# Top-k attention and two gated products: weight halves through PSUM, and an order with other costs

## The chip, the cores and the metric

One core of one Trainium2 chip runs the whole program. The metric is the device time of an execution in microseconds; a kernel's time is the median of its runs. Engines are named as the profile names them: PE (TensorE), DVE (VectorE), ACT (ScalarE), POOL (GpSimd), SP (the queue that issues the DMAs).

## The reference

```python
# q, k, v: 4 batches x 8 heads x 576 positions x 64, float32
scores = q @ k.T / sqrt(64)
kth    = 32nd largest of each row of scores           # top_k = 32
scores = where(scores >= kth, scores, -1e9)
attn   = softmax(scores)
x      = (attn @ v), heads side by side               # 2304 tokens x 512
h = x @ w_in;  g = h * sigmoid(1.702 * h);  x2 = g @ w_out        # 512 -> 2048 -> 512
a = x2 @ w1;  b = x2 @ w2;  out = ((a * b) @ w3) @ w_out2         # 512 -> 1024 -> 1024 -> 512
```

The weights arrive as 64-bit floats, the tensors q, k and v as 32-bit ones.

## The kernel before

The 2304 tokens are 18 tiles of 128 rows. A tile has 8 heads of attention, and then the two gated blocks ("the MoE part" of the code), whose products are all done with numbers split into two 16-bit halves, hi and lo: a product of two such numbers is three 16-bit matmuls, hi by hi, hi by lo and lo by hi (lines 488 to 490).

A head: four matmuls fill a score tile `s_ps` (line 706; two such tiles exist). DVE then finds the 32 largest of 576 by four MAX8 (line 728) with three MATCH_REPLACE8 between them (line 731). ACT masks and exponentiates (746, 749) with a bias `nb` from POOL or DVE (738), writes the hi half (755), POOL writes the lo half (758, 759), a DMA transposes both, and nine matmuls multiply with v (769). ACT and DVE add the halves into `xsb` (809, 813). At the end of a tile the row sums are inverted: three small DVE steps, `+1e-9` (854), reciprocal (855) and a multiplication with the scale of v (834); then `x mul` (838) scales the rows.

The weights have to be made ready first, while the first tiles' heads run. There are 72 blocks of 128 x 512: 8 of w4 (the second w_out), 16 of w3, 16 of w_in, 16 of w_out, 16 of w1 and w2. For each, a DMA brings the 64-bit words (356), ACT takes them apart in three steps (361, 371 or on POOL 366, 375), and DVE joins the words into 32-bit numbers (379, "the join": two inputs in SBUF). The Gram product of the blocks (406), its diagonal (416) and a sum (421) give one scale per matrix, six in all. Then each block is multiplied with the scale and split into halves. For 56 blocks `split_op` does it: the hi half on ACT (313), POOL (330) or DVE (316), the lo half on DVE (323, two inputs in SBUF) or on POOL in two steps (326, 327). The 16 blocks of w1 and w2 lie where their halves go, so `split_in_place` goes through a tile `fsb` (451 or 454, then 457 or 460, then 463 or 466). The halves of w3 are transposed and multiplied with those of w4 into w34 (538, 541 make its halves).

PSUM has three general banks, the pool `mm`. Products, Gram products and the small sums take one each from it.

The order of the instructions on each engine is fixed when the program is built. `Order.run` is a list scheduler: every operation has a cost, a due time and the engines it may run on; operations that are ready are taken by due time; a slot of a pool (a PSUM bank, a buffer) is taken and given back. It runs through time with `GAP` between an operation and its user on another engine, `SAME` on the same engine, and `DMA` for a transfer's flight. On the chip each engine then works through its own list strictly in that order, and waits at the head of it.

Of the kernel before, what the change touches and what calls it, by code (L numbers as in the profile page):

```python
# [35 lines left out]
class Order:  # L36
# [4 lines left out]
    GAP = 0.25  # L41
    SAME = {"T": 0.0, "V": 0.11, "A": 0.12, "G": 0.1, "D": 0.25}
    DMA = 2.3

    def __init__(self):
        self.ops = []
        self.pools = {}
        self.busy = {}
# [4 lines left out]
    def op(self, alts, due, deps=(), env=None, acq=(), rel=(), tag=""):  # L53
        o = Op()
        o.alts, o.prio = alts, due
# [11 lines left out]
    def run(self, log=None):  # L67
        engs = "TVAGD"
        free = dict.fromkeys(engs, 0.0)
        used = dict.fromkeys(engs, 0.0)  # L70
# [9 lines left out]
        while n < len(self.ops):  # L80
# [6 lines left out]
            while ends and ends[0][0] <= now:  # L87
                _, _, o = heapq.heappop(ends)
                for u in o.users:
# [3 lines left out]
                    u.ready = max(u.ready, o.end + (self.SAME[o.eng] if same else self.GAP))  # L93
# [5 lines left out]
            for e in engs:  # L99
                if free[e] > now:  # L100
                    continue
                best = None
                for c in cand[e]:
# [3 lines left out]
                    if best is not None and (o.prio, o.seq) >= (best[0].prio, best[0].seq):  # L107
                        continue
# [5 lines left out]
                    if ok:  # L114
                        best = c
# [13 lines left out]
                free[e] = now + a[1]  # L129
                used[e] += a[1]  # L130
                o.end = now + a[1] + (self.DMA if e == "D" else 0.0)
                for name, env, key in o.rel:
                    t = o.end + self.GAP
                    self.pools[name].append((t, o.seq, env[key]))
                    heapq.heappush(events, t)
# [17 lines left out]
NB_DVE = 1.0  # L153
SIGN_G = 0.5
# [7 lines left out]
def kernel(  # L162
# [38 lines left out]
    ident = mem([P, P], BF16, "ident")  # L201
# [87 lines left out]
    def dve_chain(due, fns, deps=(), env=None, acq=(), rel=(), tag=""):  # L289

        o = None
        for i, f in enumerate(fns):
            first, last = i == 0, i == len(fns) - 1
            o = dve(
                0.09, due, f, deps=deps if first else [o], env=env, acq=acq if first else [], rel=rel if last else [], tag=tag
            )
# [11 lines left out]
    def split_op(due, hi, lo, src, sc, n, deps, env, rel, acq=(), tag="", lo_dve=2.0):  # L308
# [23 lines left out]
        o = op([("A", 0.09 + 0.52 * k, f_hi, 0.0), ("G", 0.12 + 0.57 * k, f_hi_g, HI_G), ("V", 0.1 + 0.6 * k, f_hi_v, lo_dve)], due, deps=deps, env=env, acq=acq, tag=tag + "hi")  # L332
        alts = [("V", 0.1 + 0.9 * k, f_lo_v, lo_dve)]
        if lo_dve > 0.0:
            alts.append(("G", 0.4 + 1.5 * k, f_lo_g, 0.0))
# [12 lines left out]
    def load64(dst, src, raw_pool, deps):  # L348
# [34 lines left out]
        ld = dma(1.5, due - 20, f_load, deps=deps, env=E, acq=[raw_pool], tag="w load")  # L383
        lo = act(0.69, due, f_low, deps=[ld], tag="w low")
        sg = op([("A", 0.55, f_sign_a, 0.0), ("G", 0.9, f_sign, SIGN_G)], due, deps=[lo], tag="w sign")
        mn = act(0.57, due, f_main, deps=[ld, sg], tag="w main")
        return dve(0.87, due, f_join, deps=[sg, mn], env=E, rel=[raw_pool], tag="w join")
# [49 lines left out]

    def split_to(w, i, src, sc, deps):
# [5 lines left out]
    def split_in_place(w, i, sc, deps):  # L444
# [23 lines left out]
        a = op([("V", 0.67, f_v, 0.0), ("A", 0.61, f_a, 0.5)], due, deps=deps, env=E, acq=["f"], tag="w tmp")  # L468
        b = op([("A", 0.52, h_a, 0.0), ("V", 0.42, h_v, 1.0)], due, deps=[a], tag="w hi")
        return op([("G", 1.2, l_g, 0.0), ("V", 0.9, l_v, 1.5)], due, deps=[b], env=E, rel=["f"], tag="w lo")  # L470
# [4 lines left out]
    def transpose_op(due, src, acq, dep, env, n=8):  # L475
# [3 lines left out]
        return dma(1.0, due, f, deps=[dep], env=env, acq=[acq], rel=["h"], tag="T")  # L479
# [21 lines left out]
    def weights():  # L501
# [3 lines left out]
        sp4 = [split_to(wout, 8 + i, block(wout, i), s4, [d4]) for i in range(8)]  # L505
# [10 lines left out]
        for f in range(8):  # L516
# [3 lines left out]
            for kc in range(2):  # L520
                e = {}
                src = block(win, 2 * f + kc)
                s = split_op(
                    due, lambda e=e: e["h"][:, 0:C], lambda e=e: e["h"][:, C : 2 * C], lambda src=src: src, s3, C,
                    [d3], e, [], acq=["h"], tag="w3 ", lo_dve=W_DVE,
                )
# [19 lines left out]
        ready["win"] = [split_to(win, i, block(w12, i), si, [di] + sp3) for i in range(16)]  # L546
# [4 lines left out]
        ready["wout"] = [split_to(wout, i, block(w12, i), so, [do] + cout + pr) for i in range(16)]  # L551
# [5 lines left out]
        ready["w12"] = [split_in_place(w12, i, (s1, s2)[i // 8], [(d1, d2)[i // 8]]) for i in range(16)]  # L557
# [36 lines left out]
    def kv_prep(b, hp, is_v):  # L594
# [54 lines left out]
        kready[b, hp] = [dma(2.0, due, f_t, deps=[m, r], env=E, acq=["kt"], rel=["h", "kr"], tag="k T")]  # L649
# [4 lines left out]
    def q_prep(t):  # L654
# [33 lines left out]
        tr = dma(1.0, due, f_t, deps=[m], env=E, acq=[("q", E, "qa")], rel=["h"], tag="q T")  # L688
        qready[t] = [dma(1.3, due, f_swap, deps=[tr], env=E, acq=[("q", E, "qb")], tag="q swap")]


    def head(t, h, X):
# [87 lines left out]
        if first and j == 0:  # L780
            X["esc", hp] = pool(1.1 * len(pt), due - 6, f_esc(hp, hp + 1), deps=[s], tag="esc")
        elif h == 0:
            o = pool(1.1 * len(pt), due - 6, f_esc(0, NPAIR), deps=[s] + [d for b, _, _, _ in pt for i in range(NPAIR) for d in kready[b, i]], tag="esc")
# [3 lines left out]
        for i in range(3):  # L787
# [4 lines left out]
            [("G", 0.41, f_nb(nc.gpsimd), 0.0), ("V", 0.18, f_nb(nc.vector), NB_DVE)], due - 6, deps=[d, X["esc", hp]],  # L792
# [4 lines left out]
        lo = pool(1.5, due + 7, f_lo, deps=[hi], env=E, rel=["y"], tag="a lo")  # L797
        tr = dma(1.1, due + 8, f_t, deps=[lo], env=E, acq=["at"], rel=["hl"], tag="a T")
# [20 lines left out]
    def tile_end(t, X):  # L819
# [9 lines left out]
        def f_r():  # L829
            for b, s0, r0, n in pt:  # L830
# [3 lines left out]
                nc.vector.tensor_tensor(r2, r2, vi, op=ALU.mult)  # L834
# [15 lines left out]
        def f_t():  # L850
            nc.sync.dma_start_transpose(out=X["t"], in_=X["h"])

        f_rs = [
            lambda: nc.vector.tensor_scalar(r, X["x"][:, :, D], 1e-9, None, op0=ALU.add),
            lambda: nc.vector.reciprocal(r, r),
# [241 lines left out]
```

## Time and profile before

| what | value |
|---|---|
| time, median of 3 runs | 1158.55 us (1156.67 to 1162.78) |
| profiled execution | 1158.71 us, its span 1156.9 us |
| PE, DVE, ACT, POOL busy | 950.6, 960.4, 824.5, 847.8 us |
| first MAX8 of the first head | 19.9 us from the span's start |
| the last weight half | about 337 us |
| the last head's last MAX8 on DVE | about 1060 us |

The table's shares are means over three stages with different limits: up to about 337 us the weights are prepared beside the first heads, up to about 1060 us heads and MoE parts run side by side, and what is left is the MoE part of the last two tiles. A busy PE is not PE at its peak, since a matmul's time includes its way through the array: the distance between two starts tells what it occupies.

### The profile page before, as it was taken

Reading aid. Unit: us, or ns where it says so; the run is one execution under the profiler, and the core shown is the slowest. Engines: PE = TensorE matmul, PEld = TensorE weight load, DVE = VectorE, ACT = ScalarE, POOL = GpSimd, SP = SyncE. Lnnn points to the kernel's source line nnn. Section 1 sums busy time; section 2 is a strip of 40 time slices with the busy share of each in tenths; the row PEclk is TensorE's granted clock in tenths of the full one; section 3 lists DMA queues with packets and bytes.
Section 4 is the critical chain, followed back from the end, with each engine's and each line's share of the span. In section 5 each row is a group of like instructions: output and inputs, shape, how many; then the busy total and the mean of one; then the engine's idle time right before and its main releaser. Section 6 shows DMA issues by size and latency. Waiting matters only on the chain. (4 is left out here: it accounts for less than half of the span.)

```text
span 1156.9 us, 18481 instructions
## 1 busy us (share of the span) xinstructions
PE 950.6 (82%) x5654; PEld 493.7 (43%) x5654; DVE 960.4 (83%) x2112; ACT 824.5 (71%) x1555; POOL 847.8 (73%) x1142
## 2 busy tenths in 40 slices
PE   2335784556869899999889998989999999999996
PEld 1223342323435445544444544544455455555442
DVE  4887795998999888889898898899999999997311
ACT  6977769768777776877678776767868787776421
POOL 4987796657778878878688886858798787686320
PEclk9999996676979999999899998989999999999998
DMA  8959968466835846677668756666765756657331
GB/s 245 299 134 245 218 163 222 114 150 162 172 56 119 149 103 127 118 143 127 122 116 154 124 113 129 118 110 123 128 136 109 146 110 131 112 96 117 71 59 36
DMA packets 428739, 156.95 MB, mean 136 GB/s; under 512 B 406624, under 2 KB 414816, under 8 KB 428640
## 3 DMA queue, kind: packets, MB, share of 16 engines
q1 hardware_dynamic: 428640, 155.78, 65.0%
q8 instruction: 44, 0.72, 0.3%
q14 instruction: 55, 0.45, 0.1%
HBM read 52.43 MB, written 4.72 MB: 49 GB/s over the span
## 5 line engine op out<-in xcount | busy, mean ns | idle before, releaser
L728 DVE MAX8 m8s<-wsb 128x8 f32<-128x576 f32 x432 | 323.5, 754 | 5.4
L731 DVE MATCH_REPLACE8 wsb<-m8s,wsb 128x576 f32<-128x576 f32 x288 | 213.7, 742 | 0.0
L488 PE MATMUL mm<-w,tsb 128*128 128x512 f16 x432 | 167.9, 389 | 16.4 <-DMA tsb<-hsb 16.3
L488 PEld LDWEIGHTS <-tsb 128*128 128x128 f16 x1072 | 106.5, 99 | 156.6 <-DMA tsb<-hsb 47.1
L759 POOL TENSOR_TENSOR hlb<-ysb,hlb 128x512 f16<-128x512 f32 x144 | 168.1, 1168 | 0.0
L489 PE MATMUL mm<-w,tsb 128*128 128x512 f16 x432 | 167.4, 387 | 0.0
L490 PE MATMUL mm<-w,tsb 128*128 128x512 f16 x432 | 166.7, 386 | 0.0
L490 PEld LDWEIGHTS <-tsb 128*128 128x128 f16 x1072 | 106.7, 100 | 132.6 <-issue 10.6
L769 PE MATMUL av<-v2s,ats 128*128 128x130 f16 (+1 forms) x1440 | 114.1, 235 | 49.5 <-DMA ats<-hlb 40.4
L489 PEld LDWEIGHTS <-tsb 128*128 128x128 f16 x1072 | 106.6, 99 | 110.9 <-issue 13.1
L488 PE MATMUL mm<-wout,tsb 128*128 128x512 f16 x352 | 136.1, 387 | 19.7 <-DMA tsb<-hsb 16.7
L728 DVE MAX8 m8s<-s_ps 128x8 f32<-128x576 f32 x144 | 108.8, 756 | 47.4 <-PE s_ps L706 38.9
L746 ACT ACTIVATE s_ps<-s_ps,m8s 128x576 f32<-128x576 f32 x144 | 102.4, 711 | 54.7 <-DVE m8s L728 45.8
L749 ACT ACTIVATE ysb<-s_ps,nbs,asm 128x576 f32<-128x576 f32 x144 | 119.6, 831 | 28.3 <-DVE nbs L738 13.5
L490 PE MATMUL mm<-wout,tsb 128*128 128x512 f16 x352 | 136.0, 386 | 0.0
L489 PE MATMUL mm<-wout,tsb 128*128 128x512 f16 x352 | 135.9, 386 | 0.0
L769 PEld LDWEIGHTS <-ats 128*128 128x128 f16 (+1 forms) x1440 | 97.3, 108 | 82.9 <-DMA ats<-hlb 53.2
L706 PE MATMUL s_ps<-kts,qts 128*128 128x288 f16 (+1 forms) x640 | 106.8, 312 | 30.8 <-ACT ysb L749 24.7
L488 PE MATMUL mm<-win,tsb 128*128 128x512 f16 x288 | 112.4, 390 | 5.6 <-DMA tsb<-hsb 3.1
L489 PE MATMUL mm<-win,tsb 128*128 128x512 f16 x288 | 112.0, 389 | 0.0
L490 PE MATMUL mm<-win,tsb 128*128 128x512 f16 x288 | 111.8, 388 | 0.0
L918 POOL TENSOR_TENSOR fsb<-fsb 128x512 f32<-128x512 f32 x68 | 88.2, 1298 | 29.4 <-ACT fsb L909 27.1
(194 smaller groups left out, 1877.4 us busy)
## 6 DMA issues: line engine op xcount, KB each, us to landing
w<-in_moe_w_dram SPq DMA_DIRECT2D x16, 512.0 KB, 5.3
wout<-in_moe_w_in_dram SPq DMA_DIRECT2D x16, 512.0 KB, 5.3
wout<-in_moe_w_out_dram SPq DMA_DIRECT2D x16, 512.0 KB, 4.7
qts<-qts SPq DMA_DIRECT2D x36, 128.0 KB, 2.6
out_dram<-fsb SPq DMA_DIRECT2D x18, 256.0 KB, 2.4
w<-in_moe_w_out_dram SPq DMA_DIRECT2D x8, 512.0 KB, 5.0
psb<-in_moe_w_dram SPq DMA_DIRECT2D x8, 512.0 KB, 4.6
tsb<-in_moe_w_dram SPq DMA_DIRECT2D x8, 512.0 KB, 5.1
```

The source lines that it names most:

```text
L488: nc.tensor.matmul(o, a[:, i, :], hi, start=(first and i == 0), stop=False)
L489: nc.tensor.matmul(o, a[:, i, :], lo, start=False, stop=False)
L490: nc.tensor.matmul(o, a[:, 4 + i, :], hi, start=False, stop=(last and i == 3))
L706: nc.tensor.matmul(E["sp"][r : r + n, i], qe[q_][:, h, r : r + n], kt[:, j, i * HS : (i + 1) * HS], start=k_ == 0, stop=k_ == 1,)
L728: nc.vector.max(out=E["m8"][:, 8 * i : 8 * i + 8], in_=E["sp"] if i == 0 else E["w"])
L731: nc.vector.match_replace(out=two(E["w"]) if i == 0 else E["w"], in_to_replace=E["m8"][:, 8 * i : 8 * i + 8], in_values=E["sp"] if i == 0 ...
L746: nc.scalar.activation(E["sp"], E["sp"], AF.Prelu, bias=E["m8"][:, TOPK - 1 : TOPK], scale=-1.0, alpha=1.0 / FAR)
L749: nc.scalar.activation(two(E["y"]), E["sp"], AF.Exp, bias=E["nb"], scale=nesc)
L759: nc.gpsimd.tensor_tensor(hl()[:, S + SR : 2 * S], E["y"][:, 0:SM], hl()[:, 0:SM], op=ALU.subtract)
L769: nc.tensor.matmul(X["av", hp][r : r + n, j], E["at"][:, i, r : r + n], v2[:, j, blk, :], start=(i == 0), stop=(i == 8))
L918: nc.gpsimd.tensor_tensor(E["f"], E["f"], E["f2"], op=ALU.mult)
```

## The change

Four things are changed.

1. `split_pe` is new. It multiplies a block of a weight with an identity matrix of 32-bit floats, so that the block itself stands in a PSUM bank; ACT writes the hi half from there, and DVE the lo half. `PEP` names the matrices that go this way: all five, 72 blocks. `ident` becomes a 32-bit tile for it.
2. The three small steps of the row sums go to three engines: `+1e-9` to ACT, the reciprocal stays on DVE, the multiplication with v's scale goes to POOL.
3. `Order.run` knows a lock. Operations of POOL, and those of DVE that are marked with `od.two`, share it: one that starts while it is held is taken to last longer by what is left, and while choosing, such an operation's due time is put back by `LOCK` times that rest.
4. The costs, the gaps by engine and the flight times of DMAs that the scheduler calculates with are other numbers, so the whole order is another.

```diff
-    GAP = 0.25
+    GAP = {"T": 0.25, "V": 0.16, "A": 0.16, "G": 0.1, "D": 0.05}
-    DMA = 2.3
+    DMA = 2.1
...
+                    both = e == "G" or (e == "V" and a[2] in self.both)
+                    mine = (o.prio + (LOCK * max(lock - now, 0.0) if both else 0.0), o.seq)
...
+                cost = a[1]
+                if e == "G" or (e == "V" and a[2] in self.both):
+                    cost += max(lock - now, 0.0)
+                    lock = now + cost
...
+LOCK = 8.0
+PE_DUE, PE_OUT = 100.0, 20.0
+PEP = ("w4", "w3", "win", "wout", "w12")
...
-    ident = mem([P, P], BF16, "ident")
+    ident = mem([P, P], F32, "ident")
...
-        ld = dma(1.5, due - 20, f_load, deps=deps, env=E, acq=[raw_pool], tag="w load")
+        ld = dma(1.3, due - 20, f_load, deps=deps, env=E, acq=[raw_pool], tag="w load", lat=3.6)
...
-        return dve(0.87, due, f_join, deps=[sg, mn], env=E, rel=[raw_pool], tag="w join")
+        return dve(0.65, due, od.two(f_join), deps=[sg, mn], env=E, rel=[raw_pool], tag="w join")
...
+    def split_pe(hi, lo, src, sc, due, deps, env=None, acq=()):
+        E = {} if env is None else env
+        def f_in():
+            nc.tensor.matmul(E["mm"], ident, src(), start=True, stop=True)
+        def f_hi():
+            nc.scalar.activation(hi(), E["mm"], AF.Copy, scale=sc)
+        def f_lo():
+            nc.vector.scalar_tensor_tensor(lo(), E["mm"], sc, hi(), op0=ALU.mult, op1=ALU.subtract)
+        a = pe(0.87, due - PE_DUE, f_in, deps=deps, env=E, acq=["mm"] + list(acq), tag="w in")
+        h = act(0.58, due - PE_OUT, f_hi, deps=[a], tag="w hi")
+        return dve(0.66, due - PE_OUT, f_lo, deps=[h], env=E, rel=["mm"], tag="w lo")
...
-                nc.vector.tensor_tensor(r2, r2, vi, op=ALU.mult)
+                nc.gpsimd.tensor_tensor(r2, r2, vi, op=ALU.mult)
...
+        a = act(0.2, due, lambda: nc.scalar.activation(r, X["x"][:, :, D], AF.Copy, bias=1e-9), deps=r_in, tag="r")
+        a = dve(0.15, due, lambda: nc.vector.reciprocal(r, r), deps=[a], tag="r")
+        a = pool(0.3 * len(pt), due, f_r, deps=[a], tag="r")
...
-        lo = pool(1.5, due + 7, f_lo, deps=[hi], env=E, rel=["y"], tag="a lo")
-        tr = dma(1.1, due + 8, f_t, deps=[lo], env=E, acq=["at"], rel=["hl"], tag="a T")
+        lo = pool(1.42, due + 7, f_lo, deps=[hi], env=E, rel=["y"], tag="a lo")
+        tr = dma(1.35, due + 8, f_t, deps=[lo], env=E, acq=["at"], rel=["hl"], tag="a T")
```

The other lines of the diff are numbers of the same kind.

In the new program the instructions of `split_pe` stand at lines 459 (PE), 462 (ACT) and 465 (DVE), the join at 395, MAX8 at 782, MATCH_REPLACE8 at 785, the score matmuls at 760, the matmuls with v at 823, the lo half of w34 at 590, the row sums at 908 (ACT), 909 (DVE) and 888 (POOL).

DVE where the halves of w_in are made, before (`w_70` is the tile of the 32-bit blocks of w_in, `win` and `wout` are those of the halves, `w_71` is w34):

```order
191 L731 MATCH_REPLACE wsb<-m8s,s_ps_94 128x576
192 L316 TENSOR_SCALAR win<-w_70,wsm 128x512 x4
193 L541 SCALAR_TENSOR_TENSOR w_71<-mm_97,w_71 128x512
194 L316 TENSOR_SCALAR win<-w_70,wsm 128x512
195 L323 SCALAR_TENSOR_TENSOR win<-w_70,wsm,win 128x512
196 L813 TENSOR_TENSOR xsb<-xsb,av 128x2x64
197 L323 SCALAR_TENSOR_TENSOR win<-w_70,wsm,win 128x512 x3
198 L541 SCALAR_TENSOR_TENSOR w_71<-mm_99,w_71 128x512
199 L323 SCALAR_TENSOR_TENSOR win<-w_70,wsm,win 128x512 x6
200 L379 SCALAR_TENSOR_TENSOR w_70<-wout,w_70 128x512 x2
```

Fifteen halves stand there with no MAX8 or MATCH_REPLACE8 between them. And now, where the same halves are made:

```order
246 L465 SCALAR_TENSOR_TENSOR win<-mm_97,wsm,win 128x512
247 L782 MAX m8s<-wsb 128x8
248 L785 MATCH_REPLACE wsb<-m8s,s_ps_95 128x576
249 L465 SCALAR_TENSOR_TENSOR win<-mm_98,wsm,win 128x512
250 L465 SCALAR_TENSOR_TENSOR win<-mm_99,wsm,win 128x512
251 L782 MAX m8s<-wsb 128x8
252 L465 SCALAR_TENSOR_TENSOR win<-mm_97,wsm,win 128x512
253 L785 MATCH_REPLACE wsb<-m8s,wsb 128x576
254 L465 SCALAR_TENSOR_TENSOR win<-mm_98,wsm,win 128x512
255 L395 SCALAR_TENSOR_TENSOR w_70<-wout,w_70 128x512
```

All 16 lo halves are on DVE now, their source is a bank (`mm`), and head steps and joins stand between them.

PE at the same place of the new order, where the blocks of w_in come into the banks (`mm_97`, `mm_98` and `mm_99` are the three banks; before, PE had nothing to do with these blocks beyond their Gram product):

```order
1112 L760 MATMUL s_ps_95<-kts,qts 128x288
1113 L459 MATMUL mm_98<-w_70,ident 128x512
1114 L459 MATMUL mm_99<-w_70,ident 128x512
1115 L459 MATMUL mm_97<-w_70,ident 128x512
1116 L459 MATMUL mm_98<-w_70,ident 128x512
1117 L459 MATMUL mm_99<-w_70,ident 128x512
1118 L459 MATMUL mm_97<-w_70,ident 128x512
1119 L823 LDWEIGHTS ats
1120 L823 MATMUL av<-v2s,ats 128x130
```

Six blocks stand in a row over three banks, and a head's matmuls with v behind them: the fourth can start only when DVE has given back the first one's bank.

DVE at the row sums of the first tile, before:

```order
163 L813 TENSOR_TENSOR xsb<-xsb,av 128x2x64
164 L854 TENSOR_SCALAR asm<-xsb 128x8
165 L379 SCALAR_TENSOR_TENSOR w_70<-wout,w_70 128x512
166 L855 RECIPROCAL asm<-asm 128x8
167 L316 TENSOR_SCALAR hsb<-win,wsm 128x512
168 L834 TENSOR_TENSOR asm<-asm,kvinv 128x8
```

Now only the reciprocal is in DVE's list:

```order
156 L867 TENSOR_TENSOR xsb<-xsb,av 128x2x64
157 L785 MATCH_REPLACE wsb<-m8s,wsb 128x576
158 L909 RECIPROCAL asm<-asm 128x8
159 L782 MAX m8s<-wsb 128x8
160 L395 SCALAR_TENSOR_TENSOR w_70<-wout,w_70 128x512
```

Counted over the whole lists: when the sixth scale is formed on DVE (the diagonal of w2, the last matrix), 25 heads have been begun on DVE before, and 31 now; the last weight half on DVE comes after 32 begun heads. The signs of the 64-bit words are on ACT for 62 blocks before and for 48 now, the rest is on POOL. Of the 144 `nb` steps DVE has 64 before and 53 now. SP's list has as many DMAs as before. Of the 16 halves of w3, 11 go through the bank `mm_97`.

## Rows read from the trace of the kernel before

**Rows 1.** The page, busy time of each engine
```profile
PE 950.6 (82%) x5654; PEld 493.7 (43%) x5654; DVE 960.4 (83%) x2112; ACT 824.5 (71%) x1555; POOL 847.8 (73%) x1142
```

**Rows 2.** Windows: stretch, its us, busy us (instructions) by engine, PEclk, DMA share, GB/s
```profile
core 0: us, PE busy (x) PEld busy (x) DVE busy (x) ACT busy (x) POOL busy (x), PEclk, DMA share, GB/s
0.00:337.00 337.00, 188.02 (x1086) 101.95 (x1087) 277.86 (x545) 260.58 (x475) 251.48 (x302) 0.86 0.74 185
337.00:1060.00 723.00, 679.10 (x4179) 354.49 (x4177) 663.06 (x1527) 532.98 (x1021) 571.43 (x810) 0.97 0.66 123
848.00:1060.00 212.00, 207.03 (x1329) 109.90 (x1326) 202.99 (x457) 159.17 (x294) 164.37 (x231) 1.00 0.64 120
1060.00:1157.00 97.00, 83.49 (x393) 37.28 (x390) 19.47 (x43) 30.95 (x61) 24.87 (x31) 0.96 0.32 60
83.00:143.00 60.00, 38.86 (x234) 20.05 (x234) 44.77 (x90) 44.93 (x75) 41.83 (x50) 0.97 1.02 224
214.00:270.00 56.00, 28.93 (x161) 15.72 (x160) 52.91 (x102) 37.49 (x69) 42.48 (x53) 0.65 0.64 154
```

**Rows 3.** Waits of DVE from 337 to 1060: us, times, longest us
```profile
DVE m8s L728 <- PE s_ps L706: 31.7, 28, 3.8
```

**Rows 4.** DVE busy us up to 337, weight halves: L316, L323, L451, L460, L466
```profile
0.00:337.00 337.00, 13.87 (x18) 0.86 0.74 185
...
0.00:337.00 337.00, 30.63 (x25) 0.86 0.74 185
...
0.00:337.00 337.00, 7.87 (x11) 0.86 0.74 185
...
0.00:337.00 337.00, 2.76 (x4) 0.86 0.74 185
...
0.00:337.00 337.00, 1.98 (x3) 0.86 0.74 185
```

**Rows 5.** Groups by line: engine, op, out<-in, count | busy us, mean ns | idle
```profile
L541 DVE SCALAR_TENSOR_TENSOR w<-mm,w 128x512 f16<-128x512 f32 x8 | 5.4, 680 | 0.8 <-ACT w L538 0.8
...
L953 DVE SCALAR_TENSOR_TENSOR hsb<-mm,msm,hsb 128x512 f16<-128x512 f32 x18 | 13.3, 740 | 2.7 <-ACT hsb L950 2.7
...
L323 DVE SCALAR_TENSOR_TENSOR wout<-w,wsm,wout 128x512 f16<-128x512 f32 x10 | 13.2, 1386 | 0.0
```

**Rows 6.** DVE up to 337, the joins (L379)
```profile
0.00:337.00 337.00, 65.86 (x72) 0.86 0.74 185
```

**Rows 7.** The joins of w_in and w_out: duration ns min/median/max, first and last start
```profile
L379 DVE SCALAR_TENSOR_TENSOR w<-wout,w x32: 666/687/1798, 91.0 to 211.7; 128x512 uint32<-128x512 uint32 x32
```

**Rows 8.** Groups by line on DVE: row sums and the bias of the exponent
```profile
L854 DVE TENSOR_SCALAR asm<-xsb 128x8 f32<-128x8 f32 x18 | 13.3, 739 | 0.0
...
L834 DVE TENSOR_TENSOR asm<-asm,kvinv 128x8 f32<-128x8 f32 (+1 forms) x20 | 6.5, 327 | 0.1
...
L738 DVE TENSOR_SCALAR nbs<-m8s,asm 128x1 f32<-128x1 f32 x64 | 16.7, 262 | 0.7
```

**Rows 9.** Timeline, DVE: start us, us, what
```profile
330.13 3.90 DVE L854 TENSOR_SCALAR asm<-xsb 128x8 f32<-128x8 f32 x1
```

**Rows 10.** Timeline, POOL in the same stretch
```profile
331.63 1.15 POOL L463 TENSOR_TENSOR w<-fsb,w 128x512 f16<-128x512 f32 x1
332.75 1.25 POOL L995 TENSOR_TENSOR psb<-psb,fsb 128x512 f32<-128x512 f32 x1
```

**Rows 11.** Timeline, PE after the last head, two neighbours
```profile
1079.98 0.38 PE L489 MATMUL mm<-w,tsb 128*128 128x512 f16 x1
1080.19 0.38 PE L490 MATMUL mm<-w,tsb 128*128 128x512 f16 x1
```

**Rows 12.** Groups by line on ACT: a hi half from PSUM
```profile
L538 ACT ACTIVATE w<-mm 128x512 f16<-128x512 f32 x8 | 4.7, 588 | 3.8 <-PE mm L490 3.8
```

**Rows 13.** The page, the steps of a head on DVE
```profile
L728 DVE MAX8 m8s<-wsb 128x8 f32<-128x576 f32 x432 | 323.5, 754 | 5.4
L731 DVE MATCH_REPLACE8 wsb<-m8s,wsb 128x576 f32<-128x576 f32 x288 | 213.7, 742 | 0.0
```

More of the change, by code (lines that the diff above doesn't have):

```diff
@@ L92, in run @@
                     same = len(u.alts) == 1 and u.alts[0][0] == o.eng
-                    u.ready = max(u.ready, o.end + (self.SAME[o.eng] if same else self.GAP))
+                    u.ready = max(u.ready, o.end + (self.SAME[o.eng] if same else self.GAP[o.eng]))
                     if u.left == 0:
@@ L128, in run @@
                 a[2]()
-                free[e] = now + a[1]
-                used[e] += a[1]
-                o.end = now + a[1] + (self.DMA if e == "D" else 0.0)
+                cost = a[1]
+                if e == "G" or (e == "V" and a[2] in self.both):
+                    cost += max(lock - now, 0.0)
+                    lock = now + cost
+                free[e] = now + cost
+                used[e] += cost
+                o.end = now + cost + ((self.DMA if o.lat is None else o.lat) if e == "D" else 0.0)
                 for name, env, key in o.rel:
-                    t = o.end + self.GAP
+                    t = o.end + self.GAP[e]
                     self.pools[name].append((t, o.seq, env[key]))
@@ L436, in l2_scale, with split_all @@
         return inv, sc, c
+    def split_pe(hi, lo, src, sc, due, deps, env=None, acq=()):
[9 more added lines that the diff above has]
+        return dve(0.66, due - PE_OUT, f_lo, deps=[h], env=E, rel=["mm"], tag="w lo")
+    def split_all(w, first, srcs, sc, deps, name):
+        if name not in PEP:
+            return [split_to(w, first + i, src, sc, deps) for i, src in enumerate(srcs)]
+        due = CONV0 + CONV * nconv[0]
+        res = []
+        for i, src in enumerate(srcs):
+            hi, lo = halves(w, first + i)
+            res.append(split_pe(lambda hi=hi: hi, lambda lo=lo: lo, lambda src=src: src, sc, due, deps))
+        return res
     def split_to(w, i, src, sc, deps):
@@ L504, in weights @@
         i4, s4, d4 = l2_scale([block(wout, i) for i in range(8)], c4)
-        sp4 = [split_to(wout, 8 + i, block(wout, i), s4, [d4]) for i in range(8)]
+        sp4 = split_all(wout, 8, [block(wout, i) for i in range(8)], s4, [d4], "w4")
         i3, s3, d3 = l2_scale([block(win, i) for i in range(16)], c3)
@@ L545, in weights @@
         ii, si, di = l2_scale([block(w12, i) for i in range(16)], cin)
-        ready["win"] = [split_to(win, i, block(w12, i), si, [di] + sp3) for i in range(16)]
+        ready["win"] = split_all(win, 0, [block(w12, i) for i in range(16)], si, [di] + sp3, "win")
         cout = [
@@ L550, in weights @@
         io, so, do = l2_scale([block(w12, i) for i in range(16)], cout)
-        ready["wout"] = [split_to(wout, i, block(w12, i), so, [do] + cout + pr) for i in range(16)]
+        ready["wout"] = split_all(wout, 0, [block(w12, i) for i in range(16)], so, [do] + cout + pr, "wout")
         srcs = [rows(w, i, j) for w in (w1, w2) for j in range(NP_) for i in range(KB)]
@@ L556, in weights @@
         i2, s2, d2 = l2_scale([block(w12, 8 + i) for i in range(8)], c12[8:])
-        ready["w12"] = [split_in_place(w12, i, (s1, s2)[i // 8], [(d1, d2)[i // 8]]) for i in range(16)]
+        ready["w12"] = []
+        for k_, (s_, d_) in enumerate(((s1, d1), (s2, d2))):
+            if "w12" in PEP:
+                ready["w12"] += split_all(w12, 8 * k_, [block(w12, 8 * k_ + i) for i in range(8)], s_, [d_], "w12")
+            else:
+                ready["w12"] += [split_in_place(w12, 8 * k_ + i, s_, [d_]) for i in range(8)]
         c_in, c_x2, c_out = wcol(), wcol(), wcol()
```

84 lines of the change are left out of this document (44 added, 40 removed).

## The prediction

> **What bounds the kernel now.** I read the busy times first, then the windows, since a mean over the span hides that the stages have different limits, and then DVE's waits. Over the span DVE and PE are alike, 960 and 951 us [rows 1]. By stretches [rows 2]: up to 337 us, while the weights are made, nothing is full (DVE 278 of 337, which is 82%; ACT 261, POOL 251, PE 188). From 337 to 1060, with heads and MoE parts side by side, PE is busy 679 of 723 us (94%) and DVE 663 (92%), so either holds the other up; DVE's largest wait there is for score matmuls that PE does late, 31.7 us [rows 3]. In the last 212 us of this stretch they reach 97.7% and 95.8% [rows 2]. After 1060 DVE has 19 us of work in 97, and PE 83: the last tiles' products. So the end is the end of the heads plus some 97 us, and the heads end when DVE has done 941 us of work (278 and 663) in 1060. The reader is to see two things: DVE's work is the term to count, and a gain on DVE alone meets a PE that is nearly as full.
>
> **The weight halves.** Removed from DVE: 61 instructions, 13.9 + 30.6 + 7.9 + 2.8 + 2.0 = 57.1 us [rows 4]. Added: 72 lo halves from PSUM. The trace has this operation in two places, 0.680 us for w34 and 0.740 us in the MoE part [rows 5]; I take 0.71, 72 x 0.71 = 51.1 us. The bounds: 0.680 gives 49.0; if the new ones are drawn out like the lo halves from SBUF, 1.386 [rows 5], 99.8. Why those were slow is in the trace: they have two inputs in SBUF and ran beside POOL, and the same goes for the small step L854, which took 3.90 us once [rows 9], through several POOL instructions in a row [rows 10], where its mean is 0.739 [rows 8]. The form from PSUM has one input in SBUF, and its two means were taken beside a POOL that is busy three quarters of the time; so I stay near them.
>
> ACT gets 72 hi halves at 0.588 [rows 12], 42 us, and loses 30 old ones, five scalings and 14 signs, so about 10 us more in front, where it is busy 77%; I count nothing, as DVE is fuller there, and its bounds lie inside those of the rivals. POOL loses 44 lo halves and 20 hi halves; it has slack already, so this counts only through the joins below.
>
> **The identity products on PE.** There is no 32-bit matmul in the trace. A 16-bit one of 512 columns occupies 0.21 us (starts at 1079.98 and 1080.19 [rows 11]; 0.216 over a longer run). Lower bound: one such pass, 72 x 0.216 = 16 us. This kernel's own products of halves take three passes and leave lo by lo out; a full one takes four, 0.864 us, 62 us in all, which I take as the estimate. Upper bound: four passes at the lower clock. The granted clock was 0.65 as a mean from 214 to 270 [rows 2], a mix of 2.4 and 1.2 GHz; at 1.2 GHz throughout it would be 125 us. PE idles 149 of the first 337 us, so even this fits in its free time, and I cost it at nothing there. If that cover fails, it is because PE takes its list in order, which is the fourth case below.
>
> The Trainium skill, "FP8 and Floating Point Precision", section "TensorE Precision Notes", says that a true FP32 product makes four passes through the array. By that rule the estimate is the same 62 us; no run here shows it yet.
>
> **The row sums and the bias.** L854 and L834 leave DVE: 13.3 + 6.5 = 19.8 us [rows 8]. The reciprocal stays. ACT gets 18 instructions of 8 elements, none dearer than 0.588 [rows 12], under 11 us; POOL 20 short ones, none dearer than its 1.25 us [rows 10], under 25 us of 1060. In return the chain to `x mul` crosses three engines, two crossings more, at the end of a tile; the next heads run meanwhile, so I count nothing, except in the last tile (under 1 us). Of the bias steps 11 leave DVE, 11 x 0.262 = 2.9 us [rows 8].
>
> **The joins and the lock.** All 72 joins stay on DVE: 65.9 us, 0.915 each [rows 6], with a least time of 0.666 and a median of 0.687 for the largest group [rows 7]. If none met POOL, 72 x 0.687 = 49.5, a gain of 16.4 us; if the new order parts them no better, 0. POOL has 64 operations fewer in front, and the order avoids the meeting on paper; I take half, 8 us.
>
> **The sum.** DVE: -57.1 + 51.1 - 19.8 - 2.9 - 8 = -36.7 us; bounds -47.2 and +20.0. The rest of the order is new everywhere. One thing can be read from the lists: the weights are ready later by heads (the sixth scale after 31 begun heads, 25 before), so more heads are done beside the weights and the MoE parts start with a larger debt: 6 heads x 5.5 us (four MAX8 and three MATCH_REPLACE8, 4 x 0.754 + 3 x 0.742 [rows 13], and 0.2 for loads) is 33 us of DVE work moved ahead of the weights, and the MoE work of PE is pressed into fewer heads. Of DVE's 36.7 us the end can get all, if PE keeps up, or nothing, if PE's 94% is the wall. I take half, 18 us: 1158.7 (the profiled execution, 1.8 us of it outside its span) - 18 = 1140 us. The median of the runs is 1158.55, so nothing is to be corrected.
>
> **The cases.** A measurement of this kernel can tell a change of about 0.5%, 5.8 us, from none.
>
> 1. As summed: half of DVE's gain comes through. 1140, its own range 1124 to 1152. For it: DVE is the fuller engine in front, and 22 us of the gain (row sums, bias) lie in every tile. Chance 0.44.
> 2. More: the new costs also part the waits of DVE and PE on each other. From 337 to 848 DVE is busy 460 of 511 us (663 - 203 in 723 - 212), 90.0%; at the 95.8% that it has from 848 on, these 460 take 480, so 31 us less: 1109. For it: such a pace stands in the same trace, with PE at full clock. Against it: there PE is at 97.7%, and PE has the larger debt now. Chance 0.16.
> 3. PE is the wall: DVE waits for score matmuls by as much as it gained. The 31.7 us [rows 3] become 65, and the time is that of before, 1153 to 1164, say 1157. Chance 0.18.
> 4. Slower: the identity products hold up PE's list. Each waits for a bank that DVE has to give back, and score and v matmuls stand behind it. The place is the halves of w3, 11 of 16 of which go through one bank: a round is 0.864 on PE, 0.588 on ACT, 0.71 on DVE, crossings, and what stands ahead on DVE, up to two steps of a head, 1.5 us: 3.7 us before any crossing, and 4.5 at the lower clock. From 83 to 143, where these halves are made now, there are 60 us for 16 blocks [rows 2], 3.75 each; above that the stage grows. With 5 us a block it is 20 us longer, the later weights follow, and the MoE debt is never made up: 1158.7 + 20 = 1179. For it: the margin is nil. Against it: this stage is full of transfers anyway (DMA share 1.02 [rows 2]), and the scheduler knows the banks. Chance 0.22.
>
> **The numbers.** The likeliest is 1140. The range has to leave out no more than 2 in 10: half of case 2 below 1109 and two thirds of case 4 above 1172 are left out, so 1108 to 1172. Faster by over 0.5%: 0.42 of case 1, case 2, and 0.02 of case 3, together 0.60. Slower: 0.19 of case 4 and 0.02 of case 3, 0.21. Within 0.5%: the rest, 0.19.
>
> **What would show it.** L465 near 0.71 us and L459 at 0.86 us from start to start; above 1 us the one, or with a wait for DVE ahead of most of the other, speaks for case 4. The joins below 0.8 us as a mean speak for the lock's part. DVE's busy time should be near 925. The last weight half should come near 350 us with the heads further on, and the last head near 1040. If the heads end earlier and the time after them grows from 97 us, the gain went to PE's debt. If DVE's work falls and its wait for L760 grows to 65 us, it is case 3. Wrong altogether I would be if DVE's busy time did not fall.

## The result, and the profile after

| | before | after |
|---|---|---|
| time, median | 1157.61 us (1156.63 to 1162.78, 4 runs) | 1121.29 us (1119.99 to 1122.92, 4 runs) |
| ratio, 95% interval | 1 | 0.9678 [0.9646, 0.9711] |
| PE busy, and not busy in the span | 950.6, 206.3 us | 987.4, 133.7 us |
| DVE, ACT, POOL busy | 960.4, 824.5, 847.8 us | 938.6, 833.6, 755.6 us |
| granted TensorE clock, mean | 0.939 | 0.975 |
| begin of head 32 on DVE | 366.3 us | 347.5 us |
| end of the last head's last MAX8 | 1061.7 us | 1029.1 us |

The change made the kernel faster by 36.3 us, twice the forecast 18. The first line of the page after, busy time by engine, answers to [rows 1]:

```profile
PE 987.4 (88%) x5798; PEld 504.9 (45%) x5798; DVE 938.6 (84%) x2079; ACT 833.6 (74%) x1589; POOL 755.6 (67%) x1092
```

DVE lost 21.8 us of work and the time 36; PE gained 36.8 us of work, and lost 72.6 us in which it stood still. DVE stood still for 14.0 us less as well (196.5 before, 182.5 now). So DVE's work is not all that the time followed.

The windows are cut where the same work is done in both kernels, at the begin of head 32 (in the new kernel that is also the end of the weights) and at the last MAX8. Before, in three stretches (columns as in [rows 2]):

```profile
0.00:366.00 366.00, 214.81 (x1227) 114.89 (x1227) 305.74 (x607) 281.36 (x514) 274.44 (x333) 0.86 0.73 178
366.00:1061.00 695.00, 653.31 (x4045) 341.97 (x4042) 636.11 (x1466) 513.20 (x984) 549.19 (x780) 0.98 0.66 124
1061.00:1157.00 96.00, 82.49 (x388) 36.87 (x386) 18.54 (x40) 29.95 (x59) 24.14 (x30) 0.96 0.32 59
```

After, the same three:

```profile
0.00:347.00 347.00, 247.53 (x1309) 125.30 (x1310) 289.38 (x603) 287.05 (x525) 173.63 (x257) 0.94 0.78 186
347.00:1029.00 682.00, 659.78 (x4115) 343.50 (x4114) 631.78 (x1439) 517.37 (x1008) 559.13 (x806) 0.99 0.68 127
1029.00:1121.00 92.00, 80.08 (x377) 36.07 (x375) 17.45 (x39) 29.18 (x57) 22.84 (x30) 0.96 0.30 61
```

Up to head 32 DVE has 16 us less to do and the stretch is 19 us shorter, at the same busy share (83.5 and 83.4%): there the gain came through whole. From there to the last MAX8 DVE has only 4 us less, and the stretch is 13 us shorter; PE's free time in it fell from 42 to 22 us. The tail gives the last 4 us.

The new operations came at their forecast price, in the stretch up to 347 us. DVE's lo halves (L465) and joins (L395), one row each, the first for L465:

```profile
0.00:347.00 347.00, 52.54 (x72) 0.94 0.78 186
...
0.00:347.00 347.00, 62.33 (x72) 0.94 0.78 186
```

That is 0.730 and 0.866 us each (the joins 0.915 before [rows 6]). The identity product stands in PE's timeline as runs of passes, two for a block (columns: start us, us, what, passes):

```profile
169.76 1.88 PE L459 MATMUL mm<-w,ident 128*128 128x512 f32 x4
...
173.62 2.74 PE L459 MATMUL mm<-w,ident 128*128 128x512 f32 x6
```

With 0.592 for the last pass, the distance is (2.74 - 0.592) / 5 = 0.43 us a pass and 0.86 us a block, as estimated. By the rule in the Trainium skill, "FP8 and Floating Point Precision", section "TensorE Precision Notes", that a true FP32 product makes four passes, it would be an estimated 4 x 0.216 = 0.864; the time agrees, though the trace shows two instructions.

What PE waited for up to 347 us, before (waits: engine, tile and line, what ended it; us in total, times, longest):

```profile
PE av L769 <- DMA ats<-hlb: 36.3, 14, 5.3
PE mm L406 <- DVE w L379: 21.7, 17, 3.9
PE mm L406 <- DVE win L379: 18.9, 10, 3.6
PE mm L406 <- DVE wout L379: 18.7, 7, 6.6
```

and after:

```profile
...
PE mm L422 <- DVE w L395: 12.7, 7, 3.9
PE av L823 <- DMA ats<-hlb: 12.1, 8, 3.1
...
PE mm L422 <- DVE wout L395: 9.0, 2, 4.9
PE mm L422 <- DVE win L395: 8.8, 5, 3.2
```

PE's wait for joins ahead of the Gram products fell from 59 to 30.5 us, and that for the transposed attention from 36 to 12, while the identity products were added in the same stretch. From 347 to 1027 us DVE's largest wait answers to [rows 3]:

```profile
DVE m8s L782 <- PE s_ps L760: 21.0, 23, 4.1
```

### The profile page after: what moved, and what is told of

Same layout as the page of the kernel before. It is cut to its first block, busy times and chain, and to the rows that moved or that the text cites. A ratio compares the mean times of both kernels' runs of the same rounds, so it can differ in the third digit from the quotient of the medians.

```text
span 1121.1 us, 18684 instructions
## 1 busy us (share of the span) xinstructions
PE 987.4 (88%) x5798; PEld 504.9 (45%) x5798; DVE 938.6 (84%) x2079; ACT 833.6 (74%) x1589; POOL 755.6 (67%) x1092
## 4 chain that ended last, share of the span: by engine, by line
PE 38%; DVE 16%; DMA 14%; ACT 12%; POOL 12%; issue 7%; SPq 1%; POOLq 0%; ACTq 0%; DVEq 0%
PE mm L532 10%; PE mm L534 10%; PE mm L533 10%; DVE m8s L782 7%; DVE wsb L785 6%; DMA ats<-hlb 5%; DMA tsb<-hsb 5%; PE av L823 4%; PE s_ps L760 3%; POOL hsb L343 2%; POOL hlb L813 2%; ACT ysb L803 2%; POOL hsb L935 1%; ACT s_ps L800 1%; PE mm L459 1%
## 5 line engine op out<-in xcount | busy, mean ns | idle before, releaser
L532 PE MATMUL mm<-w,tsb 128*128 128x512 f16 x432 | 164.5, 381 | 12.8 <-DMA tsb<-hsb 10.2
L532 PEld LDWEIGHTS <-tsb 128*128 128x128 f16 x1072 | 105.2, 98 | 136.9 <-DMA tsb<-hsb 28.3
L534 PE MATMUL mm<-w,tsb 128*128 128x512 f16 x432 | 164.2, 380 | 0.0
L533 PE MATMUL mm<-w,tsb 128*128 128x512 f16 x432 | 164.2, 380 | 0.0
L534 PEld LDWEIGHTS <-tsb 128*128 128x128 f16 x1072 | 105.4, 98 | 128.8 <-issue 4.0
L533 PEld LDWEIGHTS <-tsb 128*128 128x128 f16 x1072 | 105.4, 98 | 116.0 <-issue 17.1
L532 PE MATMUL mm<-wout,tsb 128*128 128x512 f16 x352 | 134.0, 381 | 7.9 <-DMA tsb<-hsb 4.0
L800 ACT ACTIVATE s_ps<-s_ps,m8s 128x576 f32<-128x576 f32 x144 | 102.5, 712 | 44.6 <-DVE m8s L782 36.8
L534 PE MATMUL mm<-wout,tsb 128*128 128x512 f16 x352 | 133.9, 380 | 0.0
L533 PE MATMUL mm<-wout,tsb 128*128 128x512 f16 x352 | 133.9, 380 | 0.0
L823 PE MATMUL av<-v2s,ats 128*128 128x130 f16 (+1 forms) x1440 | 105.7, 224 | 20.2 <-DMA ats<-hlb 17.1
L760 PE MATMUL s_ps<-kts,qts 128*128 128x288 f16 (+1 forms) x640 | 101.0, 298 | 18.6 <-ACT ysb L803 15.4
L823 PEld LDWEIGHTS <-ats 128*128 128x128 f16 (+1 forms) x1440 | 90.2, 102 | 57.7 <-DMA ats<-hlb 29.6
```

The source lines that it names most:

```text
L532: nc.tensor.matmul(o, a[:, i, :], hi, start=(first and i == 0), stop=False)
L533: nc.tensor.matmul(o, a[:, i, :], lo, start=False, stop=False)
L534: nc.tensor.matmul(o, a[:, 4 + i, :], hi, start=False, stop=(last and i == 3))
L760: nc.tensor.matmul(E["sp"][r : r + n, i], qe[q_][:, h, r : r + n], kt[:, j, i * HS : (i + 1) * HS], start=k_ == 0, stop=k_ == 1,)
L800: nc.scalar.activation(E["sp"], E["sp"], AF.Prelu, bias=E["m8"][:, TOPK - 1 : TOPK], scale=-1.0, alpha=1.0 / FAR)
L823: nc.tensor.matmul(X["av", hp][r : r + n, j], E["at"][:, i, r : r + n], v2[:, j, blk, :], start=(i == 0), stop=(i == 8))
```

## The experiments

Eighteen kernels ran. Ratios are to the kernel before on the same chip, with 95% intervals; "us" in a sum is the ratio times 1157.6. H is the begin of head 32. PE's idle time counts from there to the last MAX8, unless another stretch is named. A theory's letter holds only within the expectation that names it.

### The three parts, in all eight combinations

P is the halves through PSUM, R the row sums moved, C the costs, gaps and lock. Each kernel is before with parts added, or after with parts taken back:

```diff
 # e1: before + P;  e2: before + R;  e13: before + P + R
+PEP = ("w4", "w3", "win", "wout", "w12")
...
 # e3: after without P and R;  e14: after without P
-PEP = ("w4", "w3", "win", "wout", "w12")
+PEP = ()
...
 # e5: after without R
+            lambda: nc.vector.tensor_scalar(r, X["x"][:, :, D], 1e-9, None, op0=ALU.add),
+            lambda: nc.vector.reciprocal(r, r),
+            f_r,
```

e1, expected: 

> The kernel before with the halves of all 72 weight blocks made from PSUM banks, and nothing else: row sums, costs and lock as before. Theory A (each part brings its own: the PSUM way takes DVE work and POOL's company out of the time up to head 32, 305.7 to 289.4 us of DVE work, 19 us of time; the rest came after head 32 from the order): 1135 to 1145, head 32 begun at 345 to 352 us, the stretch after it as long as before, about 694 us. Theory B (the new costs and the lock did it, by another order): 1152 to 1164, head 32 near 366. Theory C (any other order moves the time by this much, whatever the reason): anything from 1115 to 1175, and the run with one due time moved differs as much.

e2, expected: 

> The kernel before with the row sums' three small steps on ACT, DVE and POOL, and nothing else. Theory A: DVE loses 20 us of work, most of it after head 32 where DVE is 92% busy; half of it comes through, 1145 to 1152. Theory B: 1154 to 1162. Theory C: anything within 15 us of before on either side.

e3, expected: 

> The new kernel with both moves taken back: halves of the weights made as before (ACT, POOL, DVE from SBUF), row sums on DVE; the new costs, gaps and the lock stay. Theory A: 1140 to 1150, with head 32 near 366 and the stretch after it 10 to 14 us shorter. Theory B: 1120 to 1130. Theory C: anything from 1115 to 1175.

e5, expected: 

> The new kernel with the row sums back on DVE; halves from PSUM, costs and lock as in the new one. If the row sums on three engines cost time as they do in the kernel before (plus 11 us): 1108 to 1115. If they bring what they take from DVE (some 19 us of work, half of it coming through): 1128 to 1134. If the order decides more than either: 1117 to 1125.

e13, expected: 

> The kernel before with the halves through PSUM and the row sums moved, old costs and no lock. If the row sums' move pays only in an order made with the new costs: e1's 1127 plus the 11 us of e2, 1133 to 1142, with PE idle over 40 us after head 32. If it pays as soon as the halves go through PSUM: 1098 to 1121, with PE idle near 25 there.

e14, expected: 

> The changed kernel with the weights split from SBUF as before (no identity products), new costs, lock and row sums. If the row sums' move needs only the new costs: e3's 1157 minus the 29 us by which e5 is above the changed kernel, 1122 to 1134. If it needs the PSUM halves as well: 1150 to 1170.

| parts | run | median us | ratio | H us | end of last MAX8 us | PE idle us | DVE busy us |
|---|---|---|---|---|---|---|---|
| none | before | 1157.6 | 1 | 366 | 1062 | 42 | 960.4 |
| P | e1 | 1127.31 | 0.9742 [0.9716, 0.9769] | 332 | 1030 | 36 | 941.3 |
| R | e2 | 1169.83 | 1.0095 [1.0075, 1.0115] | 367 | 1075 | 51 | 941.1 |
| C | e3 | 1157.37 | 0.999 [0.9976, 1.0004] | 381 | 1058 | 31 | 954.9 |
| P, C | e5 | 1150.51 | 0.9934 [0.9912, 0.9957] | 343 | 1054 | 34 | 952.2 |
| P, R | e13 | 1123.38 | 0.9694 [0.9669, 0.9718] | 336 | 1020 | 23 | 934.2 |
| R, C | e14 | 1146.13 | 0.9891 [0.9863, 0.992] | 376 | 1054 | 34 | 942.3 |
| P, R, C | after | 1121.29 | 0.9678 [0.9646, 0.9711] | 347 | 1029 | 22 | 938.6 |

P alone brings 30 us; added to R it brings 46, to C 6, to both 25: always a gain. It brings H 29 to 38 us forward, whatever stands beside it (366 to 332, 367 to 336, 381 to 343, 376 to 347). C brings 1 us alone, -22 added to P, 24 to R, and 2 to both: with P and R the costs and the lock bring nothing that the intervals tell apart. R brings -11 alone, 6 added to P (hardly clear of the two intervals), 11 to C and 30 to both: it costs in the old order and pays where P or C is.

e1, e5, e13 and e14 lie outside every range that their expectations gave to a reading of the parts. e1 to e3 lie in the range of theory C (any other order moves the time), which e4 below contradicts.

Where P's gain comes from can be read in e1, up to H and from there to the last MAX8:

```profile
0.00:332.00 332.00, 240.98 (x1313) 123.02 (x1314) 284.87 (x611) 285.41 (x522) 171.06 (x253) 0.94 0.80 195
332.00:1029.00 697.00, 660.67 (x4102) 342.73 (x4101) 637.96 (x1467) 518.65 (x994) 556.36 (x788) 0.99 0.67 124
```

H comes 34 us earlier, with 21 us less work on DVE and 13 us less standing still; behind H nothing is gained. POOL has 103 us less to do up to H (171 instead of 274), and it makes the lo halves that the transposed attention waits for. Whether the gain is DVE's shorter work or POOL's, no run separates.

e2's two stretches show that it is not DVE's work that decided:

```profile
0.00:367.00 367.00, 216.56 (x1233) 115.55 (x1233) 296.29 (x598) 281.19 (x520) 275.79 (x336) 0.86 0.75 179
367.00:1075.00 708.00, 656.76 (x4065) 343.02 (x4062) 627.69 (x1438) 514.59 (x998) 546.96 (x792) 0.98 0.64 121
```

DVE has 19 us less to do than before, and the kernel is 11 us slower; from head 32 on DVE stands still for 80 us (59 before). Its wait for score matmuls is the largest row of this, from 345 to 1055 us, where the kernel before has 31.7:

```profile
DVE m8s L728 <- PE s_ps L706: 45.6, 34, 4.0
```

With P and R together PE's idle time after H is 22 or 23 us, with P alone or P and C 34 to 36. But e13 gains little on e1, since what its heads won (10 us) its tail gave back: 105 us, with PE busy 93.

### Is e5's 1150 an accident of the order?

```diff
-PE_DUE, PE_OUT = 100.0, 20.0
+PE_DUE, PE_OUT = 100.0, 19.0
```

The same edit in the changed kernel (e4), and in e5's (e12).

e4, expected: 

> The new kernel with PE_OUT 19 in place of 20: the due time of the weight halves' two last steps is 1 us later in the scheduler, which means nothing by itself but gives another order. Theories A and B: within 5 us of the new kernel, 1116 to 1127. Theory C: more than 10 us away from it.

e12, expected: 

> The changed kernel with the row sums back on DVE (1150.5 us) and PE_OUT 19 instead of 20, which alone moved the changed kernel by 1.4 us. If the row sums' place itself costs the 29 us, the time is 1145 to 1156. If the 1150.5 was one unlucky order among many, it comes back towards the others, 1120 to 1140.

e4: 1119.87 us, 0.9671 [0.9652, 0.969]. e12: 1150.92, 0.996 [0.9942, 0.9977]. So this small push moves neither, and the 30 us between e5 and the changed kernel (33 between e12 and e4) belong to the row sums' place in this order. e5's stretches:

```profile
0.00:343.00 343.00, 245.90 (x1291) 124.57 (x1292) 286.82 (x604) 278.55 (x506) 172.37 (x258) 0.93 0.78 188
343.00:1054.00 711.00, 677.05 (x4144) 348.90 (x4144) 644.37 (x1471) 523.92 (x1009) 566.17 (x801) 0.99 0.65 122
```

The loss is all after H: 711 us instead of 682. PE is busy 17 us longer there and idle 12 us longer, and DVE's wait for score matmuls from 345 to 1055 is

```profile
DVE m8s L782 <- PE s_ps L760: 39.0, 28, 3.6
```

where the changed kernel has 21.0. Part of PE's longer work is that more of it falls into this stretch (4144 matmuls instead of 4115); the granted clock, 0.99 in both rows, leaves little to explain. Why three short steps have this effect, and the reverse one in e2, is not settled.

### The lock, and old costs for the weights

```diff
 # e6: the lock is never held
-                    lock = now + cost
+                    lock = 0.0
...
 # e7, e8: operations of the weights and of the first four tiles get before's costs, gaps and no lock
+        od.old = t < 4
```

e7 has the row sums on DVE, e8 has them moved.

e6, expected: 

> The new kernel with the lock never held in the scheduler: the costs, gaps, halves from PSUM and row sums stay. The joins meet POOL as they fall. If the lock does what it is meant for, the joins go from 0.87 to over 0.92 us each as a mean and head 32 comes 3 to 10 us later: 1124 to 1132. If the lock delays joins and POOL's preparation of k and v (one reason why the first scale comes at 53 us and not at 39): head 32 at 335 to 342, 1108 to 1116. If it does nothing: 1117 to 1124.

e7, expected: 

> Halves from PSUM, row sums on DVE. The scheduler calculates with the costs, gaps and flight times of the kernel before, and without the lock, for the weights, for the preparation of q, k and v of the first batch and for the first four tiles, and with the new ones and the lock from the fifth tile on (32 heads). Theory: the two sets of numbers act on two stretches, the new ones make the stretch up to head 32 some 15 us longer (331.7 with the halves from PSUM alone, 347.5 in the new kernel) and the one after it 15 us shorter (698 and 682 us up to the heads' end): head 32 at 330 to 334, then 680 to 685, in all 1108 to 1115. Rival: the order is one piece and a change in one place moves all of it: 1120 to 1135.

e8, expected: 

> As the run with old costs up to head 32, with the row sums on three engines. If they cost 11 us as in the kernel before: 11 us above that run. If they bring half of what they take from DVE: 8 us below it, 1100 to 1107.

e6: 1127.28 us, 0.9729 [0.9714, 0.9745]; joins 60.5 us (62.3 with the lock), H at 329. The lock does not make the joins shorter. Without it H comes 18 us earlier, and more than that is lost behind H: the lock's 6 us lie there. e7: 1128.86, 0.9733 [0.9708, 0.9758]; e8: 1125.85, 0.9713 [0.9692, 0.9733]. H came at 329 and 334, as hoped, but the rest took 701 and 698 us instead of 682: an earlier head 32 was given back. R brings 2 us between e7 and e8, neither the loss of 11 nor the gain of 8 that was expected. In e1, e4, e6, e7, e8 and the changed kernel the last MAX8 lies between 1027 and 1032, with H anywhere from 329 to 350; e13 (1020) and e5 (1054) are outside.

### What sets the pace after head 32

The order stays that of the changed kernel, and work is left out. e9 leaves out lo by hi in three of four row blocks of the first MoE product of 16 tiles, e10 the third MATCH_REPLACE8 in every second head from tile 4 on, e18 both:

```diff
+                if tag != "h" or i == 3:
                     nc.tensor.matmul(o, a[:, 4 + i, :], hi, start=False, stop=(last and i == 3))
...
         def f_mr(i):
+            if i == 2 and t >= 4 and h % 2:
+                return
```

e9, expected: 

> The changed kernel, its order unchanged, without the product lo by hi in three of four row blocks of the first MoE product, for the first 16 tiles: 12 x 16 matmuls of 0.216 us, 41.5 us of PE's work left out (the result lacks that term). Theory A (once the halves are ready PE sets the pace: 658 busy of 680 us after head 32): the time falls by most of it, 30 to 41 us, to 1080 to 1091, and DVE's wait for score matmuls (21 us after head 32) falls below 12. Theory B (DVE sets it, 630 of 680): within 6 us of 1121. Theory C (the two hold each other up): about half, 1095 to 1110.

e10, expected: 

> The changed kernel, its order unchanged, without the third MATCH_REPLACE8 of every second head from tile 4 on: 56 x 0.742 us, 41.6 us of DVE's work left out (those heads then keep too many scores). Theory A (PE sets the pace after head 32): within 6 us of 1121, and DVE's wait for score matmuls grows from 21 to about 60. Theory B (DVE sets it): 30 to 41 us faster, 1080 to 1091. Theory C (coupled): 1095 to 1110.

e18, expected: 

> e9 and e10 in one kernel, order unchanged: 41.5 us of PE's work and 41.6 us of DVE's left out after head 32. If PE and DVE bound each other there, so that each alone gave little: 1080 to 1092, 30 to 41 us below the changed kernel. If a third thing (transfers, ACT, the order's own waits) is the bound beside them: about the sum of the two, 1102 to 1110.

e9: 1110.17 us, 0.961 [0.9588, 0.9633]. e10: 1116.91, 0.9683 [0.9632, 0.9733], the ratio of the changed kernel. e18: 1108.33, 0.9586 [0.957, 0.9603]. By the ratios, 41.5 us less on PE (by the count of matmuls some 35 of them after H) bring 8 us, 41.6 less on DVE nothing that its interval of 6 us to either side tells apart, both together 11. The profiled execution of e10 took 1128 us, 11 more than its median, so its row is that of the longest of its four. e9 lies at the edge of theory C's range, e10 in theory A's, though DVE's wait grew to 43.5 us and not to 60, and e18 in that of its second reading.

The stretch after H in e9, e10 and e18:

```profile
343.00:1015.00 672.00, 631.26 (x3954) 326.33 (x3952) 631.25 (x1441) 517.31 (x1009) 559.38 (x806) 1.00 0.68 129
```
```profile
350.00:1032.00 682.00, 661.34 (x4099) 344.33 (x4097) 588.55 (x1326) 516.39 (x1006) 558.48 (x804) 0.99 0.68 127
```
```profile
343.00:1012.00 669.00, 627.93 (x3935) 324.88 (x3934) 589.25 (x1326) 515.43 (x1005) 558.77 (x804) 1.00 0.69 129
```

In e18 PE is free 41 of 669 us and DVE 80, and still each waits for the other side. Its waits there, DVE's and then PE's:

```profile
DVE m8s L783 <- PE s_ps L761: 37.2, 38, 3.7
DVE xsb L870 <- ACT xsb L866: 14.1, 20, 1.7
```
```profile
PE mm L532 <- DMA tsb<-hsb: 16.5, 22, 2.5
PE s_ps L761 <- ACT ysb L806: 9.2, 19, 0.8
PE av L826 <- DMA ats<-hlb: 7.5, 11, 1.5
```

and the chain of work that ended last in e18, over its whole span and by engine, goes through all of them:

```profile
PE 26%; POOL 21%; ACT 16%; DVE 15%; DMA 13%; issue 9%; SPq 0%; POOLq 0%; ACTq 0%; DVEq 0%
```

So no engine alone is the bound after H, nor PE and DVE together: most of the time taken off them came back as waits in an order made for the old durations. Whether a new order for the shorter work would give more was not tried.

### What the identity products cost

```diff
 # e11: twice
+            nc.tensor.matmul(E["mm"], ident, src(), start=True, stop=True)
             nc.tensor.matmul(E["mm"], ident, src(), start=True, stop=True)
...
 # e17: over half of the columns, the rest by two products of zeros (a 64 x 128 part of ident that holds only zeros, read as 16-bit numbers)
+            nc.tensor.matmul(E["mm"][:, 0:256], ident, src()[:, 0:256], start=True, stop=True)
+            nc.tensor.matmul(E["mm"][:, 256:384], zeros, zeros, start=True, stop=True)
+            nc.tensor.matmul(E["mm"][:, 384:512], zeros, zeros, start=True, stop=True)
...
 # e15 without "w12", e16 without "w3" in
 PEP = ("w4", "w3", "win", "wout", "w12")
```

e11, expected: 

> The changed kernel with every identity product done twice into the same bank: 72 more products, 79 us more of PE busy time, all up to head 32, where PE is busy 248 of 347 us. If PE's free time in front hides the products, the time is within 6 us of 1121 and head 32 within 5 us of 347. If they stand on the path there (PE takes its list in order, and score matmuls stand behind them), head 32 comes 40 to 79 us later and the time is 1140 to 1190.

e17, expected: 

> The changed kernel with the identity product over 256 of the 512 columns (the other half of the bank is written by two short 16-bit products of zeros, so half of each weight is zero and the result is another). PE has about 30 us less in front, all else and the order stay. If the identity products stand on the path as the second set did (33 us for 79): head 32 comes 10 to 15 us earlier than 347 and the time is 1106 to 1112. If the first set is hidden in PE's free time: within 5 us of 1121.

e15, expected: 

> The changed kernel with the 16 blocks of w1 and w2 split in place as before, so 16 of 72 identity products fewer (17.6 us of PE). DVE has 12.6 us for them that way and 11.9 from PSUM, so its work stays. If PE's time in front costs 33/79 us for each us, as the second set did: 7 us faster, 1110 to 1117. If only a surplus costs, and the first set is hidden: 1119 to 1130.

e16, expected: 

> The changed kernel with the 16 blocks of w3 split from SBUF as before, 16 of 72 identity products fewer (17.6 us of PE, up to 144 us). If PE's time in front costs: 1110 to 1117, with the third scale (144 us now) no later. If the one bank for w3 does not hold and DVE's two-input halves come back beside POOL: third and later scales 5 to 15 us later and 1125 to 1136.

e11: 1154.53 us, 0.9979 [0.9963, 0.9996]; H at 380.6, 33 us later, and the rest 680 (682). e17: 1124.35, 0.9729 [0.9704, 0.9754]; H at 349.5. e15: 1133.88, 0.9776 [0.9753, 0.9799]. e16: 1130.84, 0.9762 [0.9734, 0.9791]. A second set stands on the path. 16 blocks taken off PE cost 10 to 11 us by the ratios, in another order each time: e15 lies outside both of its ranges; e16's time lies in its second, but by that reading the scales would come later. Without w3 in the banks (e16) the fourth to sixth scales come 21 to 24 us earlier (208, 261 and 309 us instead of 229, 286 and 330) and H only 4; what lies behind H takes 11 us longer. Up to H, e11 and then e17:

```profile
0.00:380.60 380.60, 302.40 (x1455) 152.89 (x1456) 293.98 (x603) 291.07 (x525) 173.37 (x257) 0.96 0.68 171
```
```profile
0.00:349.00 349.00, 249.40 (x1454) 134.80 (x1455) 288.65 (x603) 288.23 (x525) 173.73 (x257) 0.90 0.76 185
```

PE is busy 55 us longer up to H in e11, not the 79 of its expectation, and H comes 33 later. In e17 PE is busy as long as with the whole set (249 and 248 us). Two things lie behind this. The granted clock is 0.90 instead of 0.94. And the edit took little off PE: from the start of one block to the next it shows

```profile
174.19 0.59 PE L460 MATMUL mm<-w,ident 128*128 128x256 f32 x2
...
174.93 0.70 PE L460 MATMUL mm<-w,ident 128*128 128x256 f32 x2
...
175.77 0.70 PE L460 MATMUL mm<-w,ident 128*128 128x256 f32 x2
```

which is 0.74 and 0.84 us a block, against 0.86 for the whole product. That makes 1 to 9 us for 72 blocks (an estimate from these starts) and not the 30 that its expectation counted on. So e17 does not tell whether the first set costs time.

## Why the forecast came out wrong

- **The step that failed** is "Of DVE's 36.7 us the end can get all, if PE keeps up, or nothing, if PE's 94% is the wall. I take half, 18 us". It lets DVE's work shrink and half of the gain be lost again in waits. DVE's busy time fell by 21.8, all of that came through, and DVE's waits fell too, by 14.0: together the 35.8 us between the two profiles. On PE the same 35.8 are 36.8 us more work and 72.6 less standing still. e1 shows the waits falling with the halves alone (DVE's work -19.1, its waits -14.0). DVE's work alone does not do it: in e2 it fell by 19 and the time rose by 11. Why the waits go down in one order and up in another stays open.
- **The range** held the time, but not by the reasons in it: 1121 is just below the range of case 1 and short of case 2's 1109. What the range left out adds up to 0.23 (0.08 and 0.15), a little more than the 2 in 10 that it names.
- **Where the 36 us are.** 19 up to head 32, where DVE's work fell by 16; 13 from there to the last MAX8, with PE's idle time down from 42 to 22, where the forecast saw a possible wall; 4 in the tail. Shown by e1 and e13: the halves through PSUM bring 30 of the 36 by themselves, with the old costs, and 35 with the row sums.
- **The term DVE -36.7** was too large by 15. The joins gave 3.5 us instead of 8 (0.866 each, above the 0.8 that was to show the lock's part). If each DVE instruction is counted only up to the next one's start, the row sums were 17.4 us instead of 19.8, and the exchange of halves brought 3.4 instead of 6.0; the rest is spread. P and R took 19.1 and 19.3 us off DVE alone, but 26.2 together (e13). The lock's part is not there: the joins are shorter without it (e6).
- **The halves**, 0.71 forecast, 0.73 measured, and **the identity product**, 0.864 and 0.86, were right. That PE's free time covers all 72 products at no cost is not shown: e17 took too little off PE. e11 shows that it does not cover a second set.
- **The row sums** were counted as 19.8 us of DVE's work and nothing else. Their worth is -11 to +30 us by the order around them, through waits that the sum does not contain.
- **"The MoE parts start with a larger debt"** held (32 heads begun at the last half; 4115 matmuls between H and the last MAX8 instead of 4045), and the debt did no harm: PE's 20 us less of standing still there cover it.
- **Case 2** (1109) had the right direction, but its reason falls: the new costs alone bring 1 us (e3), and with P and R 2. **Case 3**, PE as the wall: DVE's wait for score matmuls fell to 21 instead of growing to 65. **Case 4** was half right. The halves of w3 took longer, from 90 to 169 us (4.9 us a block, near the 5 that it priced) instead of 86 to 150, and the sixth scale came at 330 us instead of 313. DVE's lo halves of w3, and the last ones that POOL made before:

```profile
L465 DVE SCALAR_TENSOR_TENSOR hsb<-mm,wsm,hsb x16: 733/746/753, 92.2 to 168.2; 128x512 f16<-128x512 f32 x16
...
L327 POOL TENSOR_TENSOR hsb<-win,hsb x13: 1151/1162/1677, 89.4 to 149.0; 128x512 f16<-128x512 f32 x13
```

But the kernel was not slower for it: more heads were done meanwhile (31 begun at the sixth scale instead of 25), and H came 19 us earlier.
- The last half came at 346 us (350 forecast), the last MAX8 at 1029 (1040), the tail was 92 (97).

## What to carry to other kernels

Where engines with fixed lists hold each other up, don't price a change by one engine's busy time: ask also which waits, on every engine, the change fills or opens. Here up to head 32 PE stood still for 151 us before and 99.5 now, with the identity products in between, and DVE's waits fell as well. Such free time has an end: a second identity set put head 32 back by 33 us. Make sure by the trace that a run took off an engine what it was meant to take off, as e17 did not. Test parts in combination, since one that loses alone (the row sums, 11 us) can win beside another (30 us).

## What the runs showed of the hardware

- A 32-bit product of 128 x 512 is two passes 0.43 us apart, four times a 16-bit one's time in all. Each pass loads its weights anew, in 190 ns by the median.
- In one order, up to head 32, the granted clock was 0.90 with half of the identity products, 0.94 with all and 0.96 with two sets: more work on PE, and a higher share of 2.4 GHz against 1.2. These are one profile each, and with half of them the products of zeros had changed PE's work too, so what the clock alone was worth is not shown.
- The lo half whose source is a PSUM bank took 733 to 753 ns in all 16 blocks of w3. With both inputs in SBUF, in the kernel before, one of w_in took 740 to 1646 ns.
